# A planner that keeps the four score products of a step together, half of attention's copies on VectorE, and bias tiles scaled by head

## The chip, the cores and the metric

One core of a Trainium2 chip. The metric is the device time of one execution in microseconds (us), the median of several runs; less is better. TensorE multiplies (PE in the profile, PEld its weight loads), VectorE is DVE, ScalarE is ACT, GpSimd is POOL, SyncE (SP) issues all DMAs.

## The reference, cut to what matters

```
scores = q k^T / 8                       # 4 batches, 8 heads, 576 positions, 64 per head
scores = where(0 <= rel < 128, scores - slope[h] * rel, -1e9)    # slope[h] = 2^-(h+1)
attn   = softmax(scores) @ v
x      = attn, heads side by side        # 2304 rows of 512
P      = exp(x @ w_gate - max), normalised 8 times over rows and over columns
y      = sum_e P[:, e] * (relu(x @ w1[e]) @ w2[e])               # 8 experts, 512 -> 1024 -> 512
out    = leaky_relu(y @ w_in) @ w_out                            # float64 weights, 512 -> 2048 -> 512
```

## The kernel before, in words

The 2304 rows are 18 tiles of 128. **Attention** goes over 36 steps: a tile `i` and a half of its heads, `quad` (four heads). `load_qk` fetches queries and keys; GpSimd multiplies the queries by `qscale` (minus 1/8 divided by the head's slope) into `qs`, since the bias tile `dist` holds the bare distance and the slope is applied to the sum. `scores` makes four products into two PSUM tiles `s[0]` and `s[1]`: the heads with r=0 have their 64 rows in partitions 0 to 63, those with r=1 in 64 to 127, and the program alternates between r=0 and r=1. Each fp32 product is two instructions in the trace, so a step has eight. VectorE then adds the bias and takes the row minimum (four instructions, line 504), ScalarE makes four exponentials with row sums (line 508), TensorE transposes them (`probs_T`, line 576) into `pt`, ScalarE copies two `pt` to `pb` (line 578), and `values` multiplies them with v (line 591). Tiles that lie on the border of two sequences, or on a certain tile behind it, use `dist_c` or `dist_d`. Where the window has one block of keys, a step's products have 128 columns and not 256.

**The experts and the last two layers** are 20 chunks of 512 hidden columns. Each runs over five groups of tiles (`PAIRS`), with one level of Strassen's scheme (7 products for 8) and every fp16 product made of three (high and low parts): lines 1011 and 1127. Some of the first chunk's work, and the preparation of weights, is filled in between attention's steps. While chunks 1 to 11 run, `to_single` converts the float64 weights to fp32 in 32 jobs, three to a chunk (lines 940 to 964; line 946 joins sign and exponent on VectorE, from two tensors in SBUF).

**Order.** The program's own order is only a proposal. At the end `Plan` reads all instructions, groups some into nodes that stay together, works out what each depends on and which buffers it opens, gives each a cost in ns and a latest time (`deadlines`, formerly the head of `order`), and then simulates the engines: at each step an engine takes, of what is ready, the node with the earliest latest time. The order found is imposed on every engine, TensorE and the DMA issues of SP included. On TensorE, instructions join a node while they follow each other in the program and write the same PSUM tile:

```
key = "fixed" if fixed else writes[0][0] if eng == "PE" else None
```

Scores alternate between two PSUM tiles, so that each of the four products is a node by itself.

Of the kernel before, what the change touches and what calls it, by code (L numbers as in the profile page):

```python
# [29 lines left out]
class Plan:  # L30
# [6 lines left out]

    START = {"PE": 0, "DVE": 84, "Activation": 103, "Pool": 48, "SP": 0}
    TO = {"PE": 52, "DVE": 34, "Activation": 34, "Pool": 78, "SP": 60}
    FROM_PE = 203  # L40
    LANDING = 2000.0
    PER_NS = 230.0
    NEAR = 60.0

    def __init__(self, nc, tc, slots, before, after):
        self.tc = tc
        self.nodes = []
        last = None
        for ins in nc.cur_bb.bb.instructions:
            kind = type(ins).__name__  # L50
            if kind.startswith("BassTile"):
                continue
            eng = str(ins.engine).split(".")[-1]
            reads, writes = self.operands(ins.ins), self.operands(ins.outs)
            fixed = eng == "Pool" and kind not in ("InstTensorTensor", "InstTensorCopy")
            key = "fixed" if fixed else writes[0][0] if eng == "PE" else None
            if key is not None and last is not None and (last["eng"], last["key"]) == (eng, key):
                node = last
            else:
                node = dict(eng=eng, key=key, ins=[], reads=[], writes=[], cost=0.0, landing=0.0, shared=False)  # L60
# [6 lines left out]
        self.depend(slots, before, after)  # L67

    @staticmethod
    def operands(aps):  # L70
        found = []
        for x in aps:
            ap = getattr(x, "bass_ap", None)
            if ap is None:
                continue
            dims = [(int(s), int(n)) for s, n in x.ap]
            size = {"float16": 2, "bfloat16": 2}.get(str(x.dtype).split(".")[-1], 4)
            count = 1
            for _, n in dims[1:]:
                count *= n  # L80
            found.append((ap.tensor.name, dims, int(ap.offset), size, count, str(x.dtype).split(".")[-1]))
        return found

# [21 lines left out]
    def weigh(self, node, kind, reads, writes):  # L105
        eng = node["eng"]
        kinds = [r[5] for r in reads]
        n = max([x[4] for x in reads + writes] or [1])
        lone = sum(1 for r in reads[1:] if r[4] == 1)
        if "DMA" in kind:  # L110
            sizes = [x[1][0][1] * x[4] * x[3] for x in reads + writes if x[0].split("_")[0] != "in"]
            node["cost"], node["landing"] = max(sizes) / self.PER_NS, self.LANDING
        elif eng == "PE":
            cols, wide, rows = writes[0][4], "float32" in kinds, reads[-1][1][0][1]
            if not wide:
                cost = cols / 2.4 + 2.5 if cols >= 100 else 30.0
            elif cols >= 200:
                cost = 267.0
            elif rows == 64 and cols == 128:
                cost = 160.0  # L120
            else:
                cost = 130.0 if reads[-1][4] == 64 else 109.0
            node["cost"] += cost
        elif eng == "Activation":
            node["cost"] = 230.0 if n <= 20 else 165 + 0.85 * n + 95 * (lone > 0) + 115 * (len(writes) > 1)
        elif eng == "DVE":
            banked = any(r[0].startswith(self.banked) for r in reads)
            full = [r for r in reads if r[4] > 1]
            if n <= 20:
                node["cost"] = 145.0  # L130
            elif kind == "InstTensorReduce":
                node["cost"] = 140 + 1.0 * n
            elif kind == "InstTensorScalarPtr" and len(full) == 1 and not banked:
                node["cost"], node["shared"] = 150 + 0.52 * n + 50 * (lone > 0), True
            else:
                node["cost"] = 150 + 1.04 * n + 50 * (lone > 0)
        elif eng == "Pool":
            node["cost"] += 190 + 1.89 * n if "float16" in kinds else 180 + 2.12 * n
# [8 lines left out]
    def depend(self, slots, before, after):  # L147
# [8 lines left out]
        self.whole = {name for name, pool in pool_of.items() if pool.startswith("ps_")}  # L156
# [3 lines left out]
        for i, node in enumerate(self.nodes):  # L160
# [49 lines left out]
            starts -= found  # L210

    def order(self):
        nodes = self.nodes
        n = len(nodes)
        behind, soft = [[] for _ in nodes], [[] for _ in nodes]
        for i, node in enumerate(nodes):
            for k in node["before"] | node["starts"]:
                behind[k].append(i)
            for k in node["soft"]:
                soft[k].append(i)  # L220
        ends, t = [0.0] * n, 0.0
        for i, node in enumerate(nodes):
            if node["eng"] == "PE":
                t += node["cost"]
            ends[i] = t
        latest = [0.0] * n
        for i in reversed(range(n)):
            a = nodes[i]
            latest[i] = min([latest[k] - nodes[k]["cost"] + (a["cost"] if i in nodes[k]["starts"] else -self.latency(a, nodes[k]))
                             for k in behind[i] + soft[i]]  # L230
                            + [ends[i] if a["eng"] == "PE" else t + 5000])
# [9 lines left out]
        closed = dict.fromkeys(self.users, 0.0)  # L241

        def since(i):

            t = ready[i]
            for tag, _ in nodes[i]["opens"]:
                if not empty[tag]:
                    return None
                t = max(t, min(empty[tag]))
            return t  # L250

        gpsimd = (0.0, 0.0)
        for _ in range(n):
# [9 lines left out]
            cost = nodes[pick]["cost"]  # L263
            if eng in ("DVE", "Activation", "Pool"):

                for i in sorted((i for i in at if i != pick and at[i] < t + cost), key=lambda i: latest[i]):
                    c = nodes[i]["cost"]
                    if (latest[i] < latest[pick] and max(at[i], t + cost) + c > latest[i]
                            and max(at[i], t) + c + cost <= latest[pick]):
                        pick, cost = i, c  # L270
                        break
            node = nodes[pick]
            start = max(t, at[pick])
            end = start + cost
            if node["shared"] and gpsimd[0] <= start < gpsimd[1]:
                end = max(end, gpsimd[1] + 280)
            if eng == "Pool":
                gpsimd = start, end
            free[eng] = end - self.START[eng]
# [3 lines left out]
            for name in node["uses"]:  # L283
                using[name] -= 1
                closed[name] = max(closed[name], end + (self.FROM_PE if eng == "PE" else 60))
                if not using[name]:
                    empty[self.tag_of[name]].append(closed[name])
            orders[eng].append(pick)
            for k in behind[pick]:
                ready[k] = max(ready[k], start if pick in nodes[k]["starts"] else end + self.latency(node, nodes[k]))  # L290
                left[k] -= 1
                if not left[k]:
                    waiting[nodes[k]["eng"]].append(k)
        return orders

    def fix(self):
        follows = mybir.DependencyInfo(mybir.DependencyClass.NoSync, mybir.DependencyReason.DATA)
        for picks in self.order().values():
# [3 lines left out]

    banked = ("s0", "s1", "s2", "t0", "t1", "t2_", "sq", "xt", "pt", "o_", "s_", "rt", "lp", "mt", "cp", "mp", "mb")
# [3 lines left out]
def attn_moe_kernel(  # L307
# [127 lines left out]
    dist = new(ap1, [P, 2 * P], F32, name="dist")  # L435
# [5 lines left out]
    dist_c = new(ap1, [P, 2 * P], F32, name="dist_c")  # L441
    nc.gpsimd.tensor_copy(dist_c, dist)
    nc.gpsimd.memset(dist_c[64:128, 0:192], BIG)
    dist_d = new(ap1, [P, 2 * P], F32, name="dist_d")
    nc.gpsimd.tensor_copy(dist_d, dist)
    nc.gpsimd.memset(dist_d[:, 0:64], BIG)
# [6 lines left out]
    def load_qk(i):  # L453
# [10 lines left out]
        if t0 // S != (t0 + P - 1) // S:  # L464
            bias = dist_c
        elif t0 % S == S - 4 * P:
            bias = dist_d
        else:
            bias = dist
        st[i] = dict(k=k_t, qs=qs, kb=kb, bias=bias)  # L470
# [12 lines left out]
    def scores(i, quad):  # L483
# [9 lines left out]
        e = [new(ap1, [P, 2, 2 * P], F32, tag="e", bufs=5, name="e") for _ in range(2)]  # L493
# [7 lines left out]
        for r in range(2):  # L501
            for n in range(2):
                h = 4 * quad + 2 * n + r
                st["minimum"] = nc.vector.tensor_tensor_reduce(
                    out=e[r][:, n, 0:W], in0=s[r][:, n, 0:W], in1=c["bias"][:, c0:], scale=2.0 ** (-8.0 * (h + 1) / H),
# [62 lines left out]
    def probs_T(i, quad):  # L568
# [3 lines left out]
        for r in range(2):  # L572
# [5 lines left out]
            c["copied"] = nc.scalar.activation(out=pb[:, :, 0:nb, :], in_=pt[:, :, 0:nb, :], func=AF.Copy)  # L578
# [837 lines left out]
```

## Time and profile before

| | us |
|---|---|
| median of 3 runs (1874.38 to 1875.46) | 1874.41 |
| profiled execution | 1873.55 |
| its span, first to last instruction | 1871.8 |
| TensorE busy | 1828.3 (98%) |
| ScalarE busy | 1359.0 (73%) |
| VectorE busy | 1330.9 (71%) |
| GpSimd busy | 1332.9 (71%) |

Busy time is the union of an engine's instructions. Matmuls are pipelined: each is listed until its last result, and so overlaps the next. A short idle of TensorE is therefore not listed as such.

### The profile page before, as it was taken

The numbers are of one execution on the slowest core, as the hardware profiler recorded it, in microseconds if no ns is written. First come the engines' busy times: TensorE is split into PE (matmuls) and PEld (weight loads), VectorE is DVE, ScalarE is ACT, GpSimd is POOL, SyncE is SP. The second block draws the span as 40 slices with busy tenths as digits, with TensorE's granted clock in tenths as the row PEclk, the third lists the DMA queues.
The fourth block names the chain that finished last, engine by engine and source line by source line (L and its number), as shares of the span: only waits on it lengthen the run. The fifth ranks groups of instructions, "written<-read, shape, count | busy, mean of one in ns | idle before, by whom it ended". The sixth has DMA issues, their size and how long they took to land.

```text
span 1871.8 us, 45091 instructions
## 1 busy us (share of the span) xinstructions
PE 1828.3 (98%) x17542; PEld 1611.3 (86%) x17542; DVE 1330.9 (71%) x3620; ACT 1359.0 (73%) x3123; POOL 1332.9 (71%) x1168
## 2 busy tenths in 40 slices
PE   7899999999999999999999999999999999999999
PEld 5677798888888988888888988989898888989888
DVE  5756676677767777777767767666666888787877
ACT  6888878776766676676766676666676778877764
POOL 3864586877868686877868686775767786766753
PEclk9999999999999999999999999999999999999999
DMA  6443011111111211111111210101000000101002
GB/s 219 154 125 90 3 52 46 52 58 57 41 58 55 71 52 46 52 53 62 41 58 44 83 52 30 46 1 47 24 24 24 24 24 24 47 1 47 1 32 71
DMA packets 61094, 97.80 MB, mean 52 GB/s; under 512 B 4560, under 2 KB 27600, under 8 KB 60880
## 3 DMA queue, kind: packets, MB, share of 16 engines
q1 hardware_dynamic: 60880, 94.93, 15.6%
q8 instruction: 137, 2.24, 0.5%
q14 instruction: 77, 0.63, 0.1%
HBM read 81.81 MB, written 13.11 MB: 51 GB/s over the span
## 4 chain that ended last, share of the span: by engine, by line
PE 72%; POOL 11%; issue 6%; DVE 6%; ACT 4%; DMA 1%; SPq 0%; POOLq 0%; ACTq 0%; DVEq 0%
PE t L1127 34%; PE s L1011 19%; PE sq L1011 13%; POOL h L1083 3%; PE s L498 2%; POOL acc L1138 2%; POOL raw L886 2%; PE o L591 2%; PE pt L576 1%; DVE raw L946 1%; DVE acc L1140 1%; DVE s L1039 1%; POOL w L726 1%; POOL raw L960 1%; POOL raw L964 1%
## 5 line engine op out<-in xcount | busy, mean ns | idle before, releaser
L1127 PE MATMUL t<-w,h 128*128 128x256 f16 x7560 | 952.9, 273 | 12.8 <-DVE acc L1140 8.8
L1011 PEld LDWEIGHTS <-w 128*128 128x128 f16 x8400 | 756.0, 98 | 93.4 <-issue 14.1
L1127 PEld LDWEIGHTS <-h 128*128 128x128 f16 x7560 | 734.9, 98 | 104.9 <-issue 18.1
L1011 PE MATMUL s<-xp,w 128*128 128x256 f16 (+1 forms) x4872 | 589.6, 262 | 7.4 <-DVE sq L1027 3.5
L1140 DVE SCALAR_TENSOR_TENSOR acc<-t,pu,acc 128x256 f32<-128x256 f32 x866 | 403.1, 478 | 154.4 <-PE t L1127 89.5
L1083 POOL TENSOR_TENSOR h<-s,h 128x1024 f16<-128x1024 f32 x180 | 383.6, 2131 | 159.0 <-ACT h L1080 122.4
L1011 PE MATMUL sq<-xp,w 128*128 128x256 f16 (+1 forms) x3528 | 432.8, 262 | 0.1
L1138 POOL TENSOR_TENSOR acc<-acc,part 128x256 f32<-128x256 f32 x322 | 239.2, 747 | 189.2 <-ACT part L1137 131.9
L726 POOL TENSOR_TENSOR w<-raw,w 128x512 f16<-128x512 f32 x240 | 275.0, 1165 | 63.9 <-ACT w L725 62.5
L1080 ACT ACTIVATE h<-s 128x1024 f16<-128x1024 f32 x180 | 190.0, 1056 | 86.9 <-DVE s L1039 86.7
L1039 DVE SCALAR_TENSOR_TENSOR h<-sq,h 128x512 f16<-128x512 f32 x352 | 191.9, 553 | 56.0 <-ACT h L1058 45.2
L1023 ACT ACTIVATE q<-s 128x256 f32<-128x256 f32 x364 | 138.6, 381 | 128.2 <-PE s L1011 127.6
L1137 ACT ACTIVATE part<-t,pu 128x256 f32<-128x256 f32 x322 | 151.9, 472 | 67.3 <-PE t L1127 63.1
L1027 DVE SCALAR_TENSOR_TENSOR sq<-sq,q 128x256 f32<-128x256 f32 x352 | 150.0, 426 | 60.4 <-PE sq L1011 28.7
L725 ACT ACTIVATE w<-raw 128x512 f16<-128x512 f32 x240 | 148.3, 636 | 12.8 <-PE s L1011 12.6
L1027 DVE SCALAR_TENSOR_TENSOR sq<-s,q 128x256 f32<-128x256 f32 x176 | 75.8, 431 | 114.7 <-PE s L1011 79.5
L1039 DVE SCALAR_TENSOR_TENSOR s<-sq,q 128x256 f32<-128x256 f32 x352 | 133.9, 416 | 26.4 <-ACT q L1035 25.5
L1039 DVE SCALAR_TENSOR_TENSOR s<-sq,s 128x256 f32<-128x256 f32 x352 | 146.1, 415 | 0.7
L1058 ACT ACTIVATE h<-sq 128x512 f16<-128x512 f32 x176 | 104.4, 593 | 54.4 <-DVE sq L1027 46.9
L862 ACT ACTIVATE raw<-raw,sr 128x512 f32<-128x512 f32 x160 | 110.4, 717 | 1.1 <-DVE sr L717 1.0
L886 POOL TENSOR_TENSOR raw<-raw 128x512 f32<-128x512 f32 x80 | 103.9, 1299 | 0.0
L859 ACT ACTIVATE junk<-raw 128x512 bf16<-128x512 f32 x160 | 100.1, 626 | 1.9 <-DMA raw<-in_moe_w_dram 0.7
(151 smaller groups left out, 1703.1 us busy)
## 6 DMA issues: line engine op xcount, KB each, us to landing
raw<-in_moe_w_dram SPq DMA_DIRECT2D x32, 768.0 KB, 4.6
k_t<-in_k_dram SPq DMA_DIRECT2D x16, 512.0 KB, 3.7
raw<-in_moe_w_dram SPq DMA_DIRECT2D x32, 256.0 KB, 3.6
raw<-in_moe_w_in_dram SPq DMA_DIRECT2D x16, 512.0 KB, 3.7
raw<-in_moe_w_out_dram SPq DMA_DIRECT2D x16, 512.0 KB, 3.5
q_t<-in_q_dram SPq DMA_DIRECT2D x18, 256.0 KB, 3.9
acc<-in_v_dram SPq DMA_DIRECT2D x18, 256.0 KB, 4.9
v_t<-in_v_dram SPq DMA_DIRECT2D x18, 256.0 KB, 2.6
```

Source lines behind the costliest of these rows:

```text
L725: nc.scalar.activation(out=hi, in_=src, func=AF.Copy)
L726: return nc.gpsimd.tensor_tensor(out=lo, in0=src, in1=hi, op=ALU.subtract)
L886: nc.gpsimd.tensor_tensor(out=o, in0=a, in1=b, op=op)
L1011: nc.tensor.matmul(d[b][:, f, :], t[:, wp, kk, ft * P:(ft + 1) * P], XP[p][:, o, kk, xp, :], start=(i == 0 and f == 0 and j in FIRST), sto ...
L1027: nc.vector.scalar_tensor_tensor(out=block(k), in0=ps, scalar=CS, in1=q[:, k], op0=ALU.mult, op1=ALU.add)
L1039: nc.vector.scalar_tensor_tensor(out=out, in0=in0, scalar=sc, in1=in1, op0=op0, op1=op)
L1080: nc.scalar.activation(out=h[:, 3:7, 0, :], in_=d["s"], func=AF.Copy)
L1083: nc.gpsimd.tensor_tensor(out=h[:, 3:7, 1, :], in0=d["s"], in1=h[:, 3:7, 0, :], op=ALU.subtract)
L1127: nc.tensor.matmul(ps, h[:, o, hp, f, tt * P:(tt + 1) * P], w[:, wp, ft, :], start=(i == 0 and j in FIRST), stop=(i == 5), skip_group_chec ...
L1137: nc.scalar.activation(out=part, in_=ps, func=AF.Copy, scale=s)
L1138: nc.gpsimd.tensor_tensor(out=dst, in0=dst, in1=part, op=ALU.add)
L1140: nc.vector.scalar_tensor_tensor(out=dst, in0=ps, scalar=s, in1=dst, op0=ALU.mult, op1=ALU.add)
```

## The change

- `gather` groups TensorE instructions that use 64 rows in fp32 (`mode` "rows", the score products) by the tile they read first, the keys, and not by the tile they write. The four products of a step thus become one node, in the program's alternating order, which opens both `s` tiles at once.
- Costs are set anew: products of mode "rows" and "cols", a `TURN` between modes of TensorE, VectorE instructions on two SBUF tensors are `shared` with GpSimd and wait for it in the simulation (`takes`), and a DMA's issue costs less. VectorE, held up so, may take another instruction first.
- `deadlines` works backward through the graph and gives each of VectorE, ScalarE and GpSimd only so much room as one instruction at a time leaves.
- The second of each step's two copies of `pt` goes to VectorE.
- ScalarE makes eight tiles `slopes[h]` once, the distance times -8 slope; the queries go unscaled into the product, and VectorE adds the bias and multiplies by -1/8. Only in the border tiles are the queries still multiplied (in place), with a `dist` that ScalarE makes from `slopes[0]`.
- The ring of `e` tiles has four buffers in place of five; `qs` is gone.

```
-            key = "fixed" if fixed else writes[0][0] if eng == "PE" else None
+            mode = self.mode(reads, writes) if eng == "PE" else None
+            key = "fixed" if fixed else reads[0][0] if mode == "rows" else writes[0][0] if eng == "PE" else None
...
+    def mode(reads, writes):
+        if "float32" in [r[5] for r in reads]:
+            if reads[-1][1][0][1] == 64:
+                return "rows"
+            if writes[0][1][0][1] == 64:
+                return "cols"
+        return "full"
...
+    TURN = {("full", "rows"): 190, ("full", "cols"): 140, ("rows", "full"): 100, ("cols", "full"): 105,
+            ("rows", "cols"): 140, ("cols", "rows"): 190}
-    PER_NS = 230.0
+    PER_NS = 350.0
...
-            elif kind == "InstTensorScalarPtr" and len(full) == 1 and not banked:
-                node["cost"], node["shared"] = 150 + 0.52 * n + 50 * (lone > 0), True
+            elif banked:
+                cost = 150 + 1.04 * n + 55 * (lone > 0) + 12 * (writes[0][0] in self.whole)
+            elif len(full) == 1:
+                cost, node["shared"] = 150 + 0.52 * n + 35 * (lone > 0), 126
             else:
-                node["cost"] = 150 + 1.04 * n + 50 * (lone > 0)
+                cost, node["shared"] = 205 + 1.04 * n, 195
...
+        def takes(i, t):
+            if node["eng"] == "PE":
+                cost += self.TURN.get((mode, node["mode"]), 0)
+            elif node["shared"] and gpsimd[0] <= t < gpsimd[1]:
+                cost = max(cost, gpsimd[1] - t + cost - node["shared"])
...
+                if nodes[pick]["shared"] and cost > nodes[pick]["cost"] + 100:
+                    other = [i for i in at if i != pick and not nodes[i]["shared"] and at[i] <= start + 100
+                             and max(t, at[i]) + nodes[i]["cost"] + cost <= max(latest[pick], start + cost + 200)]
...
+            if eng not in ("PE", "SP"):
+                latest[i] = min(latest[i], room[eng])
+                room[eng] = latest[i] - a["cost"] + self.START[eng]
...
+    slopes = new(ap1, [P, H, 2 * P], F32, name="slopes")
+    for h in range(H):
+        nc.scalar.activation(out=slopes[:, h], in_=dist, func=AF.Copy, scale=-8.0 * 2.0 ** (-8.0 * (h + 1) / H))
...
-        qs = new(ap2, [P, NP, P], F32, tag="qs", name="qs")
-        nc.gpsimd.tensor_tensor(out=qs, in0=q_t, in1=qscale.unsqueeze(2).to_broadcast([P, NP, P]), op=ALU.mult)
+        if crossed or t0 % S == S - 4 * P:
+            bias = new(ap1, [P, 2 * P], F32, tag="dist", name="dist")
+            nc.scalar.activation(out=bias, in_=slopes[:, 0], func=AF.Copy, scale=-0.125 * 2.0 ** (8.0 / H))
...
+            nc.gpsimd.tensor_tensor(out=q_t, in0=q_t, in1=qscale.unsqueeze(2).to_broadcast([P, NP, P]), op=ALU.mult)
...
-        e = [new(ap1, [P, 2, 2 * P], F32, tag="e", bufs=5, name="e") for _ in range(2)]
+        e = [new(ap1, [P, 2, 2 * P], F32, tag="e", bufs=4, name="e") for _ in range(2)]
...
+                bias, scale = slopes[:, h], -0.125
+                if c["bias"] is not None:
+                    bias, scale = c["bias"], 2.0 ** (-8.0 * (h + 1) / H)
...
-            c["copied"] = nc.scalar.activation(out=pb[:, :, 0:nb, :], in_=pt[:, :, 0:nb, :], func=AF.Copy)
+            if r == 0:
+                nc.scalar.activation(out=pb[:, :, 0:nb, :], in_=pt[:, :, 0:nb, :], func=AF.Copy)
+            else:
+                nc.vector.tensor_copy(pb[:, :, 0:nb, :], pt[:, :, 0:nb, :])
```

## Rows read from the trace of the kernel before

**Rows 1.** The page's first part: busy us, share, instructions of each engine.
```profile
PE 1828.3 (98%) x17542; PEld 1611.3 (86%) x17542; DVE 1330.9 (71%) x3620; ACT 1359.0 (73%) x3123; POOL 1332.9 (71%) x1168
```

**Rows 2.** Attention's stretches: busy PE, PEld, DVE, ACT, POOL; clock, DMA share, GB/s.
```profile
0.00:20.00 20.00, 11.55 (x70) 8.47 (x71) 8.87 (x47) 7.87 (x28) 8.21 (x28) 1.00 0.93 315
20.00:80.00 60.00, 54.76 (x485) 39.66 (x484) 37.79 (x150) 55.55 (x165) 38.13 (x36) 0.97 0.52 168
80.00:144.00 64.00, 60.04 (x609) 46.65 (x608) 40.39 (x152) 54.40 (x164) 39.42 (x47) 1.00 0.37 112
144.00:197.00 53.00, 51.15 (x485) 37.68 (x481) 30.26 (x125) 45.90 (x144) 18.90 (x27) 1.00 0.25 76
```

**Rows 3.** TensorE's waits, whole run: us in total, times, longest.
```profile
PE t L1127 <- DVE acc L1140: 8.8, 17, 0.6
PE s L498 <- POOL qs L461: 5.0, 1, 5.0
PE s L1011 <- DVE sq L1027: 3.5, 11, 0.4
```

**Rows 4.** TensorE's timeline in attention: start us, us, what, instructions merged.
```profile
77.85 1.14 PE L498 MATMUL s<-k_t,qs 64*128 64x256 f32 x8
...
109.17 1.09 PE L591 MATMUL o<-pb,v_t 128*64 128x128 f32 x16
110.19 0.70 PE L498 MATMUL s<-k_t,qs 64*128 64x256 f32 x2
...
111.84 0.74 PE L498 MATMUL s<-k_t,qs 64*128 64x128 f32 x8
...
177.06 1.13 PE L498 MATMUL s<-k_t,qs 64*128 64x256 f32 x4
```

**Rows 5.** Groups by line and shape, 0 to 280 us: busy, mean ns | idle before.
```profile
L498 PE MATMUL s<-k_t,qs 64*128 64x256 f32 x256 | 55.1, 416 | 1.7 <-issue 1.4
L578 ACT ACTIVATE pb<-pt 128x512 f32<-128x512 f32 x64 | 36.4, 590 | 6.6 <-PE pt L576 5.7 <-PE rt L550 0.4
L461 POOL TENSOR_TENSOR qs<-q_t,qscale 128x512 f32<-128x512 f32 x18 | 18.9, 1056 | 17.8 <-PE s L498 14.3 <-DMA q_t<-in_q_dram 3.3
L599 DVE SCALAR_TENSOR_TENSOR acc<-o,srx,rb 128x512 f32<-128x512 f32 x18 | 13.5, 749 | 9.3 <-PE o L591 6.7 <-ACT rb L566 2.2 <-ACT e L508 0.4
L498 PE MATMUL s<-k_t,qs 64*128 64x128 f32 x32 | 4.3, 378 | 7.0 <-POOL qs L461 5.0 <-DVE mn L504 2.1
L552 DVE CAST turned<-rt 112x128 bf16<-112x128 f32 x12 | 3.5, 290 | 8.9 <-PE rt L550 8.8
L578 ACT ACTIVATE pb<-pt 128x256 f32<-128x256 f32 x8 | 3.0, 379 | 2.8 <-PE pt L576 2.6 <-PE rt L550 0.3
```

**Rows 6.** Line 504's instructions on border tiles: duration min/median/max ns, first and last start.
```profile
L504 DVE CUSTOM_DVE_ANT_0 e<-s,dist_c x16: 372/421/426, 47.3 to 155.7; 128x256 f32<-128x256 f32 x16
L504 DVE CUSTOM_DVE_ANT_0 e<-s,dist_d x16: 419/420/425, 54.1 to 164.8; 128x256 f32<-128x256 f32 x16
```

**Rows 7.** DMA issues: count, KB each, median us to landing.
```profile
q_t<-in_q_dram SPq DMA_DIRECT2D x18, 256.0 KB, 3.9
```

**Rows 8.** The chain that ended last: start us, us, what.
```profile
508.04 2.12 DVE raw L946
...
1100.55 2.12 DVE raw L946
...
1246.51 1.33 PE t L1127 x12
...
1412.12 1.33 PE t L1127 x12
```

**Rows 9.** Line 946, all of it; then its turn in one chunk's timeline.
```profile
L946 DVE SCALAR_TENSOR_TENSOR raw<-raw,sign x32: 740/1182/2520, 253.1 to 1125.0; 128x512 int32<-128x512 int32 x32
...
507.80 2.13 POOL L1083 TENSOR_TENSOR h<-s,h 128x1024 f16<-128x1024 f32 x1
507.96 2.52 DVE L946 SCALAR_TENSOR_TENSOR raw<-raw,sign 128x512 int32<-128x512 int32 x1
```

More of the change, by code (lines that the diff above doesn't have):

```diff
@@ L1 @@
+import heapq
 from contextlib import ExitStack
@@ L46, in __init__, with gather @@
         self.tc = tc
+        found = []
+        for ins in nc.cur_bb.bb.instructions:
+            kind = type(ins).__name__
+            if not kind.startswith("BassTile"):
+                found.append((ins, kind, str(ins.engine).split(".")[-1], self.operands(ins.ins), self.operands(ins.outs)))
+        self.gather(found, slots)
+        self.depend(slots, before, after)
+    def gather(self, found, slots):
+        self.whole = {name for (pool, _, _), names in slots.items() for name in names if pool.startswith("ps_")}
         self.nodes = []
         last = None
[L49 to L54, printed above, removed]
+        for ins, kind, eng, reads, writes in found:
+            mode = self.mode(reads, writes) if eng == "PE" else None
             fixed = eng == "Pool" and kind not in ("InstTensorTensor", "InstTensorCopy")
-            key = "fixed" if fixed else writes[0][0] if eng == "PE" else None
+            key = "fixed" if fixed else reads[0][0] if mode == "rows" else writes[0][0] if eng == "PE" else None
             if key is not None and last is not None and (last["eng"], last["key"]) == (eng, key):
@@ L59, in __init__ @@
             else:
-                node = dict(eng=eng, key=key, ins=[], reads=[], writes=[], cost=0.0, landing=0.0, shared=False)
+                node = dict(eng=eng, key=key, mode=mode, ins=[], reads=[], writes=[], cost=0.0, landing=0.0, shared=0)
                 self.nodes.append(node)
@@ L109, in weigh @@
         lone = sum(1 for r in reads[1:] if r[4] == 1)
+        full = [r for r in reads if r[4] > 1]
+        banked = any(r[0] in self.whole for r in reads)
         if "DMA" in kind:
@@ L113, in weigh @@
         elif eng == "PE":
[L114 to L120, printed above, removed]
+            cols = writes[0][4]
+            if node["mode"] == "full" and "float32" in kinds:
+                cost = 109.0 if cols >= 64 else 60.0
+            elif node["mode"] == "rows":
+                cost = cols / 1.2
+            elif node["mode"] == "cols":
+                cost = 105.0
@@ L210, in depend, with deadlines @@
             starts -= found
-    def order(self):
+        self.behind, self.softly = [[] for _ in self.nodes], [[] for _ in self.nodes]
+        for i, node in enumerate(self.nodes):
+            for k in node["before"] | node["starts"]:
+                self.behind[k].append(i)
+            for k in node["soft"]:
+                self.softly[k].append(i)
+    def deadlines(self, products):
         nodes = self.nodes
         n = len(nodes)
[L215 to L224, printed above, removed]
-            ends[i] = t
-        latest = [0.0] * n
-        for i in reversed(range(n)):
-            a = nodes[i]
-            latest[i] = min([latest[k] - nodes[k]["cost"] + (a["cost"] if i in nodes[k]["starts"] else -self.latency(a, nodes[k]))
-                             for k in behind[i] + soft[i]]
-                            + [ends[i] if a["eng"] == "PE" else t + 5000])
@@ new lines, in deadlines @@
+        ends, t, mode = {}, 0.0, "full"
+        for i in products:
+            t += nodes[i]["cost"] + self.TURN.get((mode, nodes[i]["mode"]), 0)
+            mode = nodes[i]["mode"]
+            ends[i] = t
+        latest = [ends.get(i, t + 5000) for i in range(n)]
+        left = [len(self.behind[i]) + len(self.softly[i]) for i in range(n)]
+        room = dict.fromkeys(self.START, t + 5000)
+        heap = [(-latest[i], -i) for i in range(n) if not left[i]]
+        heapq.heapify(heap)
+        while heap:
+            i = -heapq.heappop(heap)[1]
+            a = nodes[i]
+            eng = a["eng"]
+            if eng not in ("PE", "SP"):
+                latest[i] = min(latest[i], room[eng])
+                room[eng] = latest[i] - a["cost"] + self.START[eng]
+            for k in a["before"] | a["starts"] | a["soft"]:
+                b = nodes[k]
+                end = latest[i] - a["cost"] + (b["cost"] if k in a["starts"] else -self.latency(b, a))
+                latest[k] = min(latest[k], end)
+                left[k] -= (k in a["before"]) or (k in a["starts"])
+                left[k] -= k in a["soft"]
+                if not left[k]:
+                    heapq.heappush(heap, (-latest[k], -k))
@@ L297, in fix @@
         follows = mybir.DependencyInfo(mybir.DependencyClass.NoSync, mybir.DependencyReason.DATA)
-        for picks in self.order().values():
+        products = [i for i, node in enumerate(self.nodes) if node["eng"] == "PE"]
+        for picks in self.order(self.deadlines(products)).values():
             line = [ins for i in picks for ins in self.nodes[i]["ins"]]
```

104 lines of the change are left out of this document (61 added, 43 removed).

## The prediction

> **What bounds the kernel now.** I read the page's engine totals first [rows 1]: TensorE is busy 98% of the 1871.8 us span and no other engine more than 73%. So a change pays where it shortens TensorE's own list or takes away its waits, and work on other engines counts only where TensorE waits for it. The stretches of attention come second [rows 2], since most of the edits lie there: attention ends near 197 us, TensorE is busy 177.5 of these 197 us, and ScalarE is close behind (55.55 of 60 us between 20 and 80, 54.40 of the next 64, 45.90 of the next 53), VectorE far off (117.3 of 197 in all). Third, TensorE's timeline there [rows 4], for what its busy time is made of. Fourth, its list of waits [rows 3] and the chain that ended last [rows 8], for the 1,670 us behind attention. The reader should see two things: scores are run in two manners of very different price, and the middle chunks run slower than the late ones.
>
> **Scores in one node.** In the timeline, a step's eight score instructions in a row take 1.14 us; two of them alone, one product, take 0.70, and four, two products that were kept together for one PSUM tile, take 1.13 [rows 4]. So two products on different halves of the partitions run at the same time, two on the same half one after the other. The planner before, which makes a node of what writes one PSUM tile, has taken the pairs apart: in two runs a step costs 2 x 1.13 = 2.26 us, in four 4 x 0.70 = 2.80, where it can cost 1.14. The new grouping holds all four products together in the alternating order. How many steps it mends follows from the groups [rows 5]: the scores of 256 columns keep TensorE busy 55.1 us; the 64 large copies of line 578 at two a step mean 32 such steps; all in one run they would take 32 x 1.14 = 36.5. That leaves 18.6 us. The four steps of 128 columns (eight small copies) hold 4.3 us and need 4 x 0.74 = 3.0, another 1.3. Together 19.9 us, the upper bound of this term; the lower bound is nothing, if something else sets the pace.
>
> **What else could set it.** A node that opens both `s` tiles must wait until VectorE has done all four instructions of the step before; earlier one tile came free after two. With attention at 197 / 36 = 5.5 us a step, the loop would be 1.14 for the scores and 4 x 0.42 = 1.7 for VectorE [rows 4, 6], 2.8 us; a copy put between adds 0.7 and the values' run on TensorE 1.09 [rows 4], 4.6 us. It fits, with the worst queueing too.
>
> **Copies.** Half of line 578 leaves ScalarE: 32 x 0.590 + 4 x 0.379 = 20.4 us [rows 5]. VectorE's nearest rows are line 599 (512 columns from PSUM, a second operand: 749 ns) and line 552 (128 columns from PSUM, a cast: 290) [rows 5]. A plain copy of 512 lies below the first; adding 384 columns at the slope of the two rows, (749 - 290) / 384 = 1.2 ns, gives the same 749, and the second operand should cost something. I take 690, bounds 590 and 749, and 430 for the small ones: 32 x 0.69 + 4 x 0.43 = 23.8 us more on VectorE, which ends at 141 us. Could these copies be held up by GpSimd, as line 946 is [rows 9]? Line 504, which reads PSUM and one SBUF tile, shows 372 to 426 ns over all border tiles [rows 6] while GpSimd is busy 38 of 60 us [rows 2]: no such hold. The Trainium skill, SBUF — State Buffer, Who interferes with whom, says that a VectorE instruction with at most one SBUF input, outside the two-port modes, does not contend with GpSimd. The trace agrees; were it otherwise, 36 holds of 1.8 us would make VectorE the bound.
>
> **Bias tiles and queries.** ScalarE makes eight `slopes` and, in four border tiles (16 instructions each for `dist_c` and `dist_d`, eight to a tile [rows 6]), four `dist`: 12 at about 0.38 us, the price of a 256-column copy [rows 5], 4.6 us (bounds 3 and 6). Eight fall into the first microseconds, when ScalarE is busy 7.87 of 20 us [rows 2]; I cost them at nothing, and at 3 us were the first bias late. GpSimd is relieved of 14 of 18 products, 14.8 us [rows 5], in a stretch where it waits anyway: nothing. TensorE's first wait, 5.0 us for line 461 [rows 3], loses that 1.06 us, but the steps behind it wait for keys and weights still on their way: nothing, bound 1 us gained. The query's DMA must now wait for the scores, not for GpSimd; it lands in 3.9 us [rows 7], the keys' already waits so, and one tile of two steps lies between: hidden, and no more than a few waits of 1 us if not. Four `e` tiles in place of five still hold two whole steps: nothing, bound 3 us lost.
>
> **How much of the 19.9 comes through.** ScalarE has 163.7 us of work in the first 197; minus 20.4, plus 4.6 it has 147.9. If TensorE's 19.9 went entirely, attention would end near 177: ScalarE at 84% (83% now), VectorE at 141 / 177 = 80% (60% now). No engine is over its span, but TensorE would meet two busy engines where it met one, and between 20 and 80 it already stood idle 5.2 us with ScalarE at 93% [rows 2]. I take 15, bounds 5 and 22 (the 19.9 and two of those idle microseconds).
>
> **The new plan behind attention.** The chain passes line 946 at the same place of each chunk [rows 8]: from 508.04 to 1100.55 us are seven chunks of 84.64 us. Behind the conversions, from 1246.51 to 1412.12, two chunks take 82.81 each. The same products cost 1.83 us more while the conversion runs, and that lasts from 253 to 1125 us [rows 9], 10.3 chunks: 18.9 us in all. The waits bear it out: VectorE's `acc` and `sq` hold TensorE 8.8 + 3.5 us, in 28 waits [rows 3], and shorter holds are not listed. The cause that I see: line 946 lasts 740 ns at its best and 2520 at its worst, and in the chunk at 508 it starts 0.16 us behind GpSimd's line 1083 and ends after it [rows 9]; what queues behind it on VectorE is the `sq` that TensorE waits for. The old planner gave it 732 ns always; the new one makes it wait for GpSimd in its simulation and looks for another instruction to put first. The late chunks prove that the products can run without such waits. But an order by simulated times can put a wait elsewhere, so the bounds are nothing and 18.9; I take half, 9.
>
> **Sum.** 15 + 9 + 1 for other waits in attention that ScalarE's relief shortens = 25 us off the span: 1871.8 - 25 = 1846.8. The execution's own time is 1.75 us over its span, and the runs' median 0.86 over that: 1849.4, say 1849.
>
> **Rivals.** *All comes through*: 20 to 22 in attention, 15 to 18.9 in the chunks, some 37 to 40 us; 1836. For it: both are wastes in TensorE's list that the edits name. Against: both together have no slack left for a mishap. Chance 0.22, times from 1829 to 1841.
>
> *Evacuation limits attention*: ScalarE and VectorE, not TensorE, set its pace; only ScalarE's net relief of 15.8 us counts where it was the bound (20 to 80 us: ten or so steps at 0.59, about 6 us), and the chunks give 4; 1864, from 1858 to 1869. For it: ScalarE's 93% there [rows 2]. The Trainium skill, TensorEngine Tiling (Array Packing), PSUM Bottleneck, states that rule: tiling speeds TensorE, not the emptying of PSUM, which may then be the limit. Against: 84% and 80% as worked out. Chance 0.17.
>
> *The lock of both `s` tiles*: slower. If scores wait for all of VectorE's queue (two copies or line 599 between the four, loop 4.6 + 0.75 + 0.7 = 6.0 us against 5.5 a step now), TensorE idles 0.5 us a step in 36 steps, 18 us, which eats the 15 gained; with the chunks unmended and one new wait of 0.8 us in each of ten, 1885. It decides from a loop of 5.5 us. Chance 0.08.
>
> *The node does not hold*: the products still run singly, the chunks improve little, and VectorE's 23.8 us buy nothing: within 3 us of before, 1873. For it: the mode is read from the operands' shape alone. Chance 0.05.
>
> My forecast has 0.48, its own range 1841 to 1858. With the first two rivals that is 0.87 for faster by over 0.2% (3.7 us, about what a measurement of this kernel can tell from no change); within it 0.05, slower 0.08. The range takes the forecast, most of *all comes through* and most of the evacuation case: 1830 to 1867.
>
> **What would show it.** Scores in runs of eight only, and the groups of line 498 near 40 us busy; attention's end near 180; VectorE's half of the copies near 690 ns each; line 946 near 740 ns or moved off GpSimd's long product, chunk pace between 82.8 and 84.6 in the conversion's span. I am wrong if scores wait for VectorE's minimum over 0.5 us a step, if ScalarE's share in attention passes 93%, or if the chunk pace stays at 84.6.

## The result, and the profile after

The changed kernel takes 1858.0 us (median of four runs, 1853.4 to 1861.7) against 1874.4 (1874.0 to 1875.5): ratio 0.9912, interval 0.9895 to 0.9929, or 16.4 us less. Its own runs lie 8 us apart, those of before 1.4. The profiled execution took 1853.38 us, its span is 1851.6, 20.2 below that of before.

The page's engine totals after (answering to [rows 1]):

```profile
PE 1812.1 (98%) x17542; PEld 1603.7 (87%) x17542; DVE 1367.5 (74%) x3656; ACT 1348.8 (73%) x3099; POOL 1323.0 (71%) x1154
```

Attention's stretches after, in the columns of [rows 2]:

```profile
0.00:20.00 20.00, 13.50 (x89) 9.20 (x89) 10.94 (x61) 13.64 (x49) 5.29 (x22) 1.00 0.92 308
20.00:80.00 60.00, 54.92 (x557) 42.41 (x557) 51.55 (x188) 58.80 (x179) 42.31 (x43) 1.00 0.57 188
80.00:144.00 64.00, 60.02 (x602) 46.43 (x598) 48.40 (x164) 56.05 (x175) 33.99 (x40) 0.95 0.37 116
144.00:180.00 36.00, 35.62 (x439) 28.22 (x436) 27.82 (x108) 28.38 (x98) 10.69 (x18) 1.00 0.25 75
```

TensorE's busy time between 20 and 80 us is what it was, but it runs 557 matmuls in it where it ran 485. Its timeline shows why (answering to [rows 4]; line 570 is line 498 of before, line 669 is 591):

```profile
109.27 1.13 PE L570 MATMUL s<-k_t,q_t 64*128 64x256 f32 x8
112.44 1.13 PE L570 MATMUL s<-k_t,q_t 64*128 64x256 f32 x8
...
178.46 1.37 PE L669 MATMUL o<-pb,v_t 128*64 128x128 f32 x16
```

All 36 steps have their scores in whole runs (34 runs of eight instructions and one of sixteen), and the last matmul of the values starts at 179.6 us (in the last row), where before it did at 197.9. The groups of 0 to 280 us (answering to [rows 5]; lines 654 and 656 are the two halves of line 578):

```profile
L570 PE MATMUL s<-k_t,q_t 64*128 64x256 f32 x256 | 39.6, 416 | 0.8 <-DVE mn L579 0.8
L656 DVE COPY pb<-pt 128x512 f32<-128x512 f32 x32 | 21.9, 684 | 2.9 <-PE o L669 1.1 <-ACT raw L940 0.8 <-ACT q L1101 0.8
L654 ACT ACTIVATE pb<-pt 128x512 f32<-128x512 f32 x32 | 18.8, 588 | 2.3 <-PE pt L651 2.1
L570 PE MATMUL s<-k_t,q_t 64*128 64x128 f32 x32 | 4.3, 376 | 5.1 <-DMA k_t<-in_k_dram 4.4 <-DVE mn L579 0.7
```

Behind attention, two lines of the conversion (1024 is line 946 of before, [rows 9]; 1018 is line 940, `exponent()`, a shift and mask with one SBUF input):

```profile
L1018 DVE TENSOR_SCALAR raw<-raw x32: 414/650/4328, 234.1 to 1100.7; 128x512 int32<-128x512 int32 x32
L1024 DVE SCALAR_TENSOR_TENSOR raw<-raw,sign x32: 741/752/1750, 236.5 to 1101.9; 128x512 int32<-128x512 int32 x32
```

The worst of line 946 has gone from 2520 to 1750 ns. But line 1018 has a worst of 4328 ns where line 940 had 2233, and the chain that ended last passes it three times (answering to [rows 8]):

```profile
903.05 3.97 DVE raw L1018
989.63 3.98 DVE raw L1018
1076.59 4.25 DVE raw L1018
```

TensorE's waits over the whole run (answering to [rows 3]) show what this costs; the last row is of 880 to 1100 us alone:

```profile
PE s L1089 <- ACT q L1101: 10.2, 8, 2.6
PE s L570 <- DMA k_t<-in_k_dram: 4.4, 1, 4.4
...
PE s L1089 <- DVE sq L1105: 1.7, 6, 0.7
...
PE s L1089 <- ACT q L1101: 7.0, 3, 2.6
```

Before, VectorE's `acc` and `sq` held TensorE 8.8 and 3.5 us; `sq` is at 1.7 now and `acc` at 1.1, but three waits of up to 2.6 us for ScalarE's `q` are new, 7.0 us between 880 and 1100.

Where the gain was made and lost is seen by counting the fp16 matmuls of lines 1089 and 1205 (1011 and 1127 before; 798 to a chunk) and comparing when the same count starts. The 400th comes 20.7 us earlier than before (199.8 against 220.5). The first chunk behind it takes 82.2 us against 80.4, which costs 1.8 of this lead; then each takes 83.1 to 84.3, and the lead grows to 26.2 us at the 6784th (867.3 against 893.6). The next three take 86.6, 86.9 and 85.5, the ones with the three holds. At the start of the last chunk the lead is 19.6, over the whole span 20.2.

Behind one of these holds TensorE lost more than its wait. After it had stood still for 2.21 us, from 992.5, its granted clock was 0.51 of full speed for 3.4 us, the lower of its two levels (1.2 GHz in place of 2.4), where six matmuls took 1.49 us in place of 0.82:

```profile
995.60:999.00 3.40, 3.40 (x19) 2.46 (x17) 1.78 (x4) 1.87 (x4) 2.25 (x3) 0.51 0.00 0
```

Behind the holds at 903 and 1076 the clock stayed at full speed.

### What holds line 1018

The same place in two chunks of this one execution. VectorE's timeline, first where it goes well, then where it does not:

```profile
819.95 0.65 DVE L1018 TENSOR_SCALAR raw<-raw 128x512 int32<-128x512 int32 x1
...
903.05 3.96 DVE L1018 TENSOR_SCALAR raw<-raw 128x512 int32<-128x512 int32 x1
```

GpSimd's timeline at the same two places:

```profile
819.05 1.26 POOL L964 TENSOR_TENSOR t<-raw 128x512 f32<-128x512 f32 x1
820.28 2.31 POOL L1161 TENSOR_TENSOR h<-s,h 128x1024 f16<-128x1024 f32 x1
...
902.13 1.29 POOL L964 TENSOR_TENSOR t<-raw 128x512 f32<-128x512 f32 x1
903.36 2.14 POOL L1161 TENSOR_TENSOR h<-s,h 128x1024 f16<-128x1024 f32 x1
905.45 1.28 POOL L964 TENSOR_TENSOR raw<-raw,t 128x512 f32<-128x512 f32 x1
```

Both times line 1018 starts while GpSimd's line 964 is still running, 0.33 us ahead of line 1161 in the first and 0.31 in the second. In the first it goes next, ends at 820.6, and line 1161 takes 2.31 us. In the second line 1161 goes next, and the following line 964 too: line 1018 ends 0.28 us behind that one. `sq`, which stands behind it on VectorE, is late, ScalarE's next `q` with it, and TensorE stands still:

```profile
908.09 0.82 PE L1089 MATMUL s<-xp,w 128*128 128x256 f16 x6 [2.21 <-ACT q L1101]
```

The lead is not what decides, as two more places of the same execution show, VectorE's rows first and then GpSimd's: with 0.31 us line 1018 goes first, with 0.70 it does not.

```profile
485.39 0.65 DVE L1018 TENSOR_SCALAR raw<-raw 128x512 int32<-128x512 int32 x1
...
1076.50 4.33 DVE L1018 TENSOR_SCALAR raw<-raw 128x512 int32<-128x512 int32 x1
```

```profile
485.70 2.32 POOL L1161 TENSOR_TENSOR h<-s,h 128x1024 f16<-128x1024 f32 x1
...
1077.20 2.13 POOL L1161 TENSOR_TENSOR h<-s,h 128x1024 f16<-128x1024 f32 x1
```

My theory after this: the order that the plan writes out puts line 1161 close behind line 1018 in the first conversion of most chunks, and this order does not settle who goes first. (In its simulation a `shared` instruction waits for GpSimd's running product only. Line 1018, with one SBUF tensor, is `shared` too, not only those on two that the list of the change names.) The losses of a run and the spread between runs are these holds. The rivals: they belong to certain chunks; or the gain behind attention was lost to something else of the plan.

### The profile page after: what moved, and what is told of

It reads as the page before. It is cut to its first block, busy times and chain, and to the rows that moved or that the text cites. A ratio compares the mean times of both kernels' runs of the same rounds, so it can differ in the third digit from the quotient of the medians.

```text
span 1851.6 us, 45040 instructions
## 1 busy us (share of the span) xinstructions
PE 1812.1 (98%) x17542; PEld 1603.7 (87%) x17542; DVE 1367.5 (74%) x3656; ACT 1348.8 (73%) x3099; POOL 1323.0 (71%) x1154
## 4 chain that ended last, share of the span: by engine, by line
PE 76%; POOL 7%; ACT 6%; DVE 5%; DMA 4%; issue 2%; SPq 0%; POOLq 0%; DVEq 0%; ACTq 0%
PE t L1205 36%; PE s L1089 20%; PE sq L1089 15%; POOL w L804 3%; DMA raw<-in_moe_w_dram 3%; POOL h L1161 1%; PE s L570 1%; PE o L669 1%; PE pt L651 1%; ACT junk L937 1%; POOL xp L804 1%; DVE s L1117 1%; DVE raw L1018 1%; ACT raw L940 1%; DVE acc L1218 1%
## 5 line engine op out<-in xcount | busy, mean ns | idle before, releaser
L1218 DVE SCALAR_TENSOR_TENSOR acc<-t,pu,acc 128x256 f32<-128x256 f32 x866 | 407.3, 479 | 173.5 <-PE t L1205 149.9
```

The source lines that it names most:

```text
L1218: nc.vector.scalar_tensor_tensor(out=dst, in0=ps, scalar=s, in1=dst, op0=ALU.mult, op1=ALU.add)
```

## The experiments

**The same kernel again**, five runs.

> The changed kernel once more, nothing altered. Theory (a race for the SBUF port): the spread of its times comes from the chunks in which line 1018, VectorE's shift and mask of the conversion, finds GpSimd's next product already queued and waits about 4 us for two of them; each such hold costs TensorE 2.4 to 2.9 us, the profiled run had three, so a profile with n holds over 3 us takes 1846 + 2.5 n us, and the end of attention stays within 1 us of 180. Rival (the spread comes from attention, its loads above all): the number of holds stays three while attention's end moves by several us.

1854.5 us (1850.8 to 1861.2), ratio 0.9903 (0.9887 to 0.9919). VectorE's timeline in its profile:

```profile
485.63 3.61 DVE L1018 TENSOR_SCALAR raw<-raw 128x512 int32<-128x512 int32 x1 [0.27 <-DMA raw<-in_moe_w_in_dram]
...
905.72 0.64 DVE L1018 TENSOR_SCALAR raw<-raw 128x512 int32<-128x512 int32 x1
```

Line 1018 is held at 485.6, 989.6 and 1076.8 us. The chunk that had a hold at 903 has none; it took 83.9 us here, 86.6 there: under one order the same place goes both ways. The hold at 485.6 is new, and of another kind: line 1018 had waited 0.27 us for its load, and came 0.04 us behind GpSimd's product:

```profile
485.59 2.15 POOL L1161 TENSOR_TENSOR h<-s,h 128x1024 f16<-128x1024 f32 x1
```

The other two stand where they stood, and the last one stands also in the runs below with both copies on ScalarE (1078.7), with the queries scaled (1079.7) and without sharing (1085.0). So chance has a part in it, and so has the place. With three holds the expected sum is 1853.5; the profiled execution took 1854.4.

**The edit that decides it**: the plan as it is, and GpSimd's next planned instruction waits until line 1018 (line 1031 here) is done, 32 waits in all.

```
+                behind = [k for k in orders["Pool"] if self.starts[k] > self.starts[i]]
+                if behind:
+                    self.tc.add_manual_dep(self.nodes[behind[0]]["ins"][0], node["ins"][-1].name, waits, reason="port")
```

> The changed kernel with its plan as it is, and one more wait for each of the 32 conversions: the GpSimd product that the plan puts behind line 1018 (0.2 us behind it in the first conversion of most chunks) waits until that instruction is done, so that it can't come in ahead. Theory (a race for the port): no hold of line 1018 over 3 us, every conversion chunk at 83.0 to 84.0 us, 1845 to 1849 us, spread under 3 us. Rival (the holds only fill time that the chunk loses elsewhere, to loads that land late): chunks of 86 us stay and 1852 us or more.

1848.5 us (1847.3 to 1849.7), ratio 0.9863 (0.9848 to 0.9877): 6 to 9.5 us better than the two medians of the changed kernel, and a spread of 2.3 us. One chunk of it, VectorE and then GpSimd:

```profile
738.64 0.64 DVE L1031 TENSOR_SCALAR raw<-raw 128x512 int32<-128x512 int32 x1
...
740.07 2.03 DVE L1037 SCALAR_TENSOR_TENSOR raw<-raw,sign 128x512 int32<-128x512 int32 x1
```

```profile
739.42 2.13 POOL L1174 TENSOR_TENSOR h<-s,h 128x1024 f16<-128x1024 f32 x1 [0.43 <-DVE raw L1031]
```

GpSimd's product now waits 0.43 us for VectorE, and VectorE's 4 us are gone. The line over the whole run:

```profile
L1031 DVE TENSOR_SCALAR raw<-raw x32: 414/631/2072, 234.4 to 1096.0; 128x512 int32<-128x512 int32 x32
```

Behind a first chunk of 82.5, chunks take 83.5 to 84.8 us while the conversion runs; three of them lie above the 84.0 that was expected. Between 880 and 1100 us TensorE's waits for `q`, 7.0 us, are gone:

```profile
PE s L1102 <- DVE sq L1118: 1.8, 3, 0.8
```

The race is shown, and that it makes the loss. The spread shrinks with it, from 8 and 10 us to 2.3, but that the holds alone make it is not shown: they can be counted in one execution of each kernel only, and of the changed kernel's nine executions the two slowest, at 1861 us, also have the lowest granted clock (0.993 and 0.994), the fastest the highest (0.999). Line 1037, whose shortest is 740 ns, lasts 2.03 us in the same chunk, as it now meets the product that follows.

**GpSimd waits for all three of the conversion's VectorE instructions** (lines 1031, 1037, 1042), the same edit with a wider test.

> As the kernel in which GpSimd's next product waits for line 1018, and the same for the conversion's other two VectorE instructions, lines 1024 and 1029. Theory (the 0.6 us that TensorE still loses at the first conversion of a chunk is the same race): pace of the conversion chunks 82.9 to 83.4 us, 1842 to 1846 us. Rival (GpSimd, made to wait, is late itself for the products and sums behind): pace 83.8 us or more, 1848 to 1854 us.

1845.2 us (1844.1 to 1846.8), ratio 0.9850 (0.9835 to 0.9864): 3.3 us more. Attention ends 2 us later than with the first mend (181.8 against 180.1), so that all of it comes behind: after a first chunk of 82.3, chunks of 83.2 to 84.1 us up to 786 us and 83.0 to 83.3 from there to the end of the conversion. The last of the three now never waits:

```profile
L1042 DVE TENSOR_SCALAR raw<-raw x32: 408/417/423, 241.3 to 1100.8; 128x512 int32<-128x512 int32 x32
```

**The planner told of the worst case**: a `shared` instruction that meets a busy GpSimd counts as if it waited for a further product.

```
-                cost = max(cost, gpsimd[1] - t + cost - node["shared"])
+                cost = max(cost, gpsimd[1] - t + 2130 + cost - node["shared"])
```

> The changed kernel, whose planner now counts on a VectorE instruction that meets a busy GpSimd to wait for one more product of 2130 ns. Theory (the race): the planner keeps such instructions out of GpSimd's runs, no hold of line 1018 over 3 us, a chunk pace of 83.0 to 83.6 us throughout the conversion, 1845 to 1850 us with a spread of under 2. Rival (the late chunks lose to their loads, which land later than planned): two or three chunks of 86 us stay, 1852 to 1862.

1893.0 us, ratio 1.0103 (1.0090 to 1.0117). Neither forecast came near. The plan came out different everywhere: attention ends at 197.4 us, TensorE waits 6.3 us at a stretch in it, and one line 1018 lasts 9.16 us, at 340, and costs TensorE 4.8. It neither bears out the race nor speaks against it; one cost in a planner is no isolated edit.

**The grouping undone**: everything else as after, TensorE's nodes by the tile they write.

```
-            key = "fixed" if fixed else reads[0][0] if mode == "rows" else writes[0][0] if eng == "PE" else None
+            key = "fixed" if fixed else writes[0][0] if eng == "PE" else None
```

> The changed kernel with the score products in nodes by the PSUM tile they write, as before. Theory (the pairing of the scores is attention's gain): scores run singly again, attention ends 14 to 18 us later, 1871 to 1877 us. Rival (the copies moved from ScalarE are the gain): at most 6 us slower, 1856 to 1864.

1879.8 us, ratio 1.0034 (1.0021 to 1.0048), slower than before. Products stand singly again, as its timeline of TensorE shows, and their group is dearer than in [rows 5]:

```profile
152.04 0.70 PE L570 MATMUL s<-k_t,q_t 64*128 64x256 f32 x2
...
153.25 0.70 PE L570 MATMUL s<-k_t,q_t 64*128 64x256 f32 x2
```

```profile
L570 PE MATMUL s<-k_t,q_t 64*128 64x256 f32 x256 | 68.3, 426 | 0.8 <-DVE mn L579 0.4 <-POOL sx L855 0.3
```

68.3 us against 39.6 and, before, 55.1; attention ends at 204.9. The new costs and latest times take the pairs apart more often than the old ones did, so that the grouping is worth 21.8 or 25.3 us inside the new plan, by which of the changed kernel's two medians is taken. Both theories had expected less.

**The grouping alone**, on the kernel before (its choice of a time for a node counts two opened tiles).

```
-            key = "fixed" if fixed else writes[0][0] if eng == "PE" else None
+            rows = eng == "PE" and "float32" in [r[5] for r in reads] and reads[-1][1][0][1] == 64
+            key = "fixed" if fixed else reads[0][0] if rows else writes[0][0] if eng == "PE" else None
```

> The kernel before with the new grouping of the score products alone. Theory: attention ends near 182, the chunk pace of 84.6 us stays, 1857 to 1861 us. Rival (ScalarE must be relieved too before TensorE can run ahead): at most 8 us gained, 1866 to 1874.

1864.3 us (1863.7 to 1865.2), ratio 0.9952 (0.9937 to 0.9967): 9.6 us, between what the two had expected. Its scores of 256 columns are busy 39.8 us, 15.3 less than before, yet attention ends only 5 us earlier, at 192.8. Its second stretch, beside [rows 2]:

```profile
20.00:80.00 60.00, 49.82 (x469) 36.55 (x467) 42.43 (x145) 52.62 (x156) 34.41 (x33) 0.97 0.55 168
```

TensorE is busy 4.9 us less there and does no more work (469 matmuls, 485 before): the time taken out of its list became idle time in the old order.

This run also speaks on line 946, to which the prediction put down the chunks' slower pace. From the third chunk on the pace stays at 84.3 to 84.8 us while the conversion runs, yet that line (949 here) has a median of 743 ns where it had 1182 [rows 9]; its long waits have gone from most places:

```profile
L949 DVE SCALAR_TENSOR_TENSOR raw<-raw,sign x32: 732/743/2641, 248.0 to 1120.1; 128x512 int32<-128x512 int32 x32
```

The conversion's third line lasts up to 2351 ns here, 951 before. So long instances of line 946 are not needed for the slow pace.

**The same with every second copy on VectorE.**

> The kernel before with the new grouping and with every second copy on VectorE. Theory (under the old plan ScalarE keeps TensorE from running ahead): attention ends 4 to 9 us earlier than with the grouping alone, 1855 to 1860 us. Rival (the copies are worth nothing, as under the new plan): within 2 us of the grouping alone, 1862 to 1866 us.

1865.4 us (1863.7 to 1865.6), ratio 0.9954 (0.9940 to 0.9969): the same as without, as is the end of attention (192.8). So ScalarE was not what kept the grouping's gain back.

**Both copies back on ScalarE**, the rest as after.

```
-            if r == 0:
+            if r >= 0:
```

> The changed kernel with both copies of a step on ScalarE again. Theory (the paired scores pay in full only when ScalarE is relieved: the grouping alone gave the kernel before 9.6 us of the 19.4): attention ends 6 to 11 us later, 1860 to 1866 us. Rival (TensorE's list alone sets attention's length): within 2 us of the changed kernel, 1852 to 1857 us.

1856.7 us (1854.9 to 1858.1), ratio 0.9906 (0.9891 to 0.9921): between the two medians of the changed kernel. Attention ends 2 us later (181.8); line 1018 is held four times in its profile, so these 2 us may hide in the race. So the copies' move is worth about 2 us in attention at most, and nothing that the times show.

**Queries scaled by GpSimd as before**, three `dist` tiles and no `slopes`, the rest as after.

```
+        qs = new(ap2, [P, NP, P], F32, tag="qs", name="qs")
+        nc.gpsimd.tensor_tensor(out=qs, in0=q_t, in1=qscale.unsqueeze(2).to_broadcast([P, NP, P]), op=ALU.mult)
```

> The changed kernel with the queries scaled by GpSimd in every tile and the three distance tiles as before, no slopes; four e buffers stay. Theory (GpSimd had the room, and the eight tiles hide in the head): attention's end within 2 us, 1852 to 1858 us. Rival (the product between the queries' load and the scores costs TensorE at the start and in the dense steps): 3 to 8 us more, over 1858.

1861.3 us (1857.0 to 1864.3), ratio 0.9929 (0.9912 to 0.9947): 3 to 7 us worse; attention ends 6 us later (185.6). Most of that is lost in the first 15 us. VectorE's timeline there:

```profile
10.14 1.31 DVE L553 TENSOR_REDUCE vmx<-acc 128x1 f32<-128x512 f32 x2 [6.27 <-DMA acc<-in_v_dram]
11.37 0.28 DVE L576 CUSTOM_DVE_ANT_0 e<-s,dist 128x128 f32<-128x128 f32 x1
```

and TensorE's two waits in its first 20 us:

```profile
PE s L570 <- DVE mn L576: 5.8, 1, 5.8
PE s L570 <- POOL qs L533: 4.9, 1, 4.9
```

This plan puts the maximum over the values ahead of the first minima, and it must wait for its load; in the changed kernel the first minimum starts at 5.76 us:

```profile
5.76 0.29 DVE L579 CUSTOM_DVE_ANT_0 e<-s,slopes 128x128 f32<-128x128 f32 x1 [4.62 <-ACT slopes L516]
```

The second wait, the rival's, is GpSimd's product, but the changed kernel waits 4.4 us for the keys at the same place. So what the scaling is worth here is for the most part an order around one load, not GpSimd's time.

**No sharing in the planner's costs**: instructions on two SBUF tensors no longer wait for GpSimd in its simulation.

```
-                cost, node["shared"] = 205 + 1.04 * n, 195
+                cost = 205 + 1.04 * n
```

> The changed kernel, whose planner no longer lets VectorE instructions on two SBUF tensors wait for GpSimd. Theory (the chunks gain because the plan knows what line 1024, formerly 946, waits for): 2.5 us instances come back and the pace of the conversion chunks is 84.3 to 84.8 us; 1858 to 1866 us, attention's end within 3 us. Rival (the backward pass with room for one instruction at a time is the cause): the pace stays at 83.1 to 83.6 in chunks without a hold of line 1018.

1864.0 us (1860.1 to 1868.8), ratio 0.9954 (0.9937 to 0.9971), 6 to 10 us worse, with attention's end 2 us later (181.7) and chunks, from the second on, from 83.4 to 87.4 us. But line 1024 is not what came back (751 ns median, 1752 at most); line 1018, which this edit leaves `shared`, is held three times, up to 4329 ns, as often as after. So the cost does pay behind attention in this plan, though not by the instruction that I had named; like the worst case above it changes the whole order, and by which instruction it pays is not shown.

**The old latest times**, with the new costs.

```
+        for i in reversed(range(n)):
+            latest[i] = min([latest[k] - nodes[k]["cost"] + (a["cost"] if i in nodes[k]["starts"] else -self.latency(a, nodes[k]))
...
+                            + [ends[i] if a["eng"] == "PE" else t + 5000])
```

> The changed kernel, planner's costs, nodes and choices as changed, with the latest times worked out as before (no room for one instruction at a time on an engine). Theory (the 13 us of attention that the grouping alone does not bring come from the new latest times): attention ends at 187 to 194 us, 1862 to 1872 us. Rival (the new costs bring them): attention's end within 3 us of 180, 1852 to 1860 us.

1864.2 us (1862.5 to 1866.6), ratio 0.9951 (0.9936 to 0.9966). Attention ends at 186.4, the 400th matmul comes 7.2 us later than after: taken out of this plan, the new latest times cost about 7 us of attention's gain.

**The race mended, and a DMA priced as before**: the edit of the first mend, and

```
-    PER_NS = 350.0
+    PER_NS = 230.0
```

> As the kernel in which GpSimd's next product waits for line 1018, with the planner's old price of a DMA's bytes (230 per ns in place of 350). Theory (loads in the head land later than planned, 6.1 us at the median for the early values, and the old price is nearer): 1 to 4 us less than with 350, 1844 to 1848 us. Rival (the price only shuffles the order): 1848 to 1854 us.

1838.9 us (1837.4 to 1839.8), ratio 0.9817 (0.9800 to 0.9833): the best version, 35 us under the kernel before, and better than I had expected. Attention ends 2 us earlier (178.2); the other 8 come behind it, most of them in chunks of about 83.3 us where the first mend has 83.8. The rival's range, from 1848 on, is missed as well. Why a price for transfers does that there is not settled: I have no run that takes it apart.

## Why the prediction was right, and where its terms were off

The forecast was 1849 with its own range from 1841 to 1858, and 1830 to 1867 with the rivals; the time lies on the upper edge of the first and inside the second. 25 us were forecast, 16.4 measured. The sum was 16 in attention and 9 behind it. The profiled run, the fastest of the four, gave 20.7 by the 400th matmul (18.3 at the end of attention) and, behind it, lost about 1. That the total came out inside the range is in part luck: too little for attention made up for half of what was missing behind it.

Of the three signs of being wrong none came as written: waits for the minimum are 1.5 us in all, ScalarE is busy 87% of attention (156.9 of 180 us), and the pace left 84.6, with 83.1 to 84.3 in chunks without a hold.

**Scores in one node**: right. Runs of eight only (two of them back to back once), 1.13 us each where nothing holds them; the group is busy 15.5 us less (18.6 was the bound from the x8 run); the four steps of 128 columns stayed at 4.3 us, so that their 1.3 us did not come. What I had wrong is that this is a term by itself. Alone it is worth 9.6 us, taken out of the new plan 22 to 25: what it is worth depends on whether the order fills the time it frees.

**The lock of both `s` tiles**: right that it fits. TensorE's waits for the minimum (line 579) come to 1.5 us in all.

**Copies**: durations right (684 and 416 ns; I took 690 and 430), and GpSimd does not hold them: the 32 large ones on VectorE last 639 to 692 ns, with GpSimd busy 42 of 60 us between 20 and 80. The Trainium skill, SBUF — State Buffer, Who interferes with whom, says so for a VectorE instruction with at most one SBUF input outside the two-port modes, and the trace agrees. That ScalarE's relief was worth something was wrong: with or without it the time is the same within 2 us, under the new plan and under the old. ScalarE is busy 98% between 20 and 80 us, and TensorE stands idle 5.1 us there as it did before (5.2). The rival of evacuation thus describes that stretch; but with 20 us more on ScalarE attention ended only 2 us later, so ScalarE has room behind 80 us (56 of 64 us busy after, 60 with both copies), and a busy share of one stretch was a poor sign.

**Bias tiles and queries**: costed at nothing. Undone they cost 3 to 7 us, most of it by the order around the `acc` load, a wait in VectorE's queue that I had not looked for.

**The new plan in attention**: I had no term for it beyond 1 us. The old latest times give back 7 us. This and the scaling's order more than cover the 4.7 us by which attention beat its 16; prices of parts taken out one at a time do not add up to the whole.

**The new plan behind attention**: the term that failed, at two steps. The first is the cause: line 946's holds were there, and they are fewer now (median 752 ns), but they are as few with the grouping alone (743), where the pace stays at 84.3 to 84.8 us, and without the sharing (751), where it is no better. The lead did grow by 5.5 us up to 867 us; which part of the plan made it grow is open. The second is where the waits went: "an order by simulated times can put a wait elsewhere" is what happened. Line 1018 (2233 ns at worst before) was put 0.3 us ahead of a long product. The three chunks with holds took 5.0 us of the lead again, the later ones 1.6. With the race taken out the same order gives 1848.5, with all three instructions guarded 1845.2. "I take half, 9" held the risk as a smaller gain; it belonged into the sum as a loss per chunk with a chance.

## What to carry to other kernels

A plan of times that puts two engines' instructions on one port within some tenths of a microsecond has not ordered them. If the loser of the race pays more than the winner's duration, write the order as a dependency: 32 of them, of which 14 made GpSimd wait in the profiled run, 13 by under half a microsecond and one by 3.0, bought 6 to 9.5 us here. And take out one part of a planner's change at a time before giving each a price: the grouping was worth 9.6 us or 22 to 25, the copies next to nothing, the latest times 7.

## What the runs showed of the hardware

An instruction of VectorE with one SBUF input, 414 ns for 512 columns at its shortest, waited for GpSimd's running product and, in the bad case, for the two behind it too, 3.96 us in place of 0.65, though it stood ready 0.31 us before the first of these two started. A longer lead does not save it: in the same execution it went first with leads of 0.31 and 0.33 us and went last with 0.31 and 0.70. The Trainium skill, SBUF — State Buffer, Who interferes with whom, says that a VectorE instruction in a two-port mode contends with GpSimd, names `tensor_scalar` among those that can enter one, and says that whoever issues first gets the shared ports for the whole instruction while the other blocks fully. The trace agrees as to the blocking: line 1018 ends 0.28 us behind the last of GpSimd's products. As to who goes first it does not, since line 1018 stood ready first and went behind. Which mode line 1018 ran in, no view shows, and how the next holder is chosen stays open.
